# The sums of a block move into the weights' narrowing tile, the block tiles are loaded two blocks ahead, and the last weight pair is prepared in a fixed hand-out over four units

## The chip, the cores and the metric

The kernel runs on one core of one Trainium2 chip. The metric is the device time of one execution in microseconds. The time of a kernel is the median of several runs; a profiled execution is a run of its own, with its own time.

## The reference

Three stages follow one another. The change touches only the end of the third.

```python
# 1. retention (linear attention with decay), B, H, S, D = 4, 8, 768, 64
for t in range(S):
    state = gamma * state + einsum('bhd,bhe->bhde', k[:, :, t], v[:, :, t])
    y[:, :, t] = scale * einsum('bhd,bhde->bhe', q[:, :, t], state)
x = y.transpose(0, 2, 1, 3).reshape(3072, 512)
# 2. soft mixture of experts: 8 experts of 4 slots, softmax over tokens in, over slots out
logits = x @ phi
x = softmax_rows(logits) @ experts(softmax_columns(logits).T @ x)
# 3. two-layer network, 3072 tokens, 512 -> 2048 -> 512
h = x @ w_in
out = (h * sigmoid(1.702 * h)) @ w_out
```

## The kernel before

The third stage works on six blocks b = 0 to 5 of 512 tokens and on sixteen column groups of the 2048 hidden columns. A float32 product is split into high and low parts of a shorter type, and three matmuls (high by high, high by low, low by high) make one product.

The first column groups of each block are multiplied in the plain way, in the "plain units". Their result, 512 x 512 per block, goes by ScalarE into the tile stage and by DMA into a DRAM buffer parts[b].

The remaining column groups are taken in pairs r, one pair per "s-unit", and each pair is multiplied by a scheme of seven products instead of eight (the functions around s_unit, product and quad). There are 31 s-units n = 0 to 30: six per block in blocks 0 to 2, five in blocks 3 and 4, three in block 5. One s-unit is 42 matmuls of 128 x 256 (line 712) and two matmuls into the PSUM bank hb (line 678), which make the hidden values of the units that come next. ScalarE turns hb into the tile forms (line 680), casts the high parts ha and hs (line 696) and VectorE makes sums of forms and the low parts la and ls (line 673, the helper vadd). These are always one unit ahead of TensorE. The seven products of a block gather in PSUM over its units. In the last unit of a block VectorE and ScalarE combine them into the tile pt[b], which was loaded from parts[b]; the combination needs four sums e of 128 x 512, which are kept in a tile of their own, ev[b]. The first of them, e[:, 0], is a copy by ScalarE (line 756) that stands in the middle of the last unit, ahead of the cast of hs and of the next activation. The last four additions of a block, pt[b] plus a sum, are deferred: finish_block puts them on a list, and each of the block's successors' units takes one of them (in block 5 two). After the second and the fourth, store sends half a block, 512 KB, to the output.

The pool wq has three buffers (NQ = 3). They hold raw weights until VectorE has narrowed them, and after that the tiles pt and ev in turn. A new tile may be written only when every use of the tile that had the buffer has ended, DMA transfers too. All transfers of this stage are issued on SyncE's queue in the order in which the program names them.

The weights of pair 7, the last one, are prepared during the first s-units. VectorE narrows them into the tile wf["a"] (six instructions of lines 165 to 169), makes three sums, ScalarE casts two high halves (line 608) and VectorE subtracts two low halves (out tile wo_hl). What is emitted after which unit is set by work(budget), which takes from a queue until the costs written beside the items use up the budget of 1.7 (BUDS); after the fourth unit it takes all that is left. The tile wf["a"] serves pairs 2, 4, 6 and 7 and has no use after pair 7. Items of the list raws load the next raw tile each time that one has been narrowed; the last three items are load_part(0), make_ev(0) and load_part(1).

The order of instructions on each engine is the order in which the program is written.

Of the kernel before, what the change touches and what calls it, by code (L numbers as in the profile page):

```python
# [7 lines left out]
F32 = mybir.dt.float32  # L8
# [14 lines left out]
P = 128  # L23
# [9 lines left out]
NB = NT // 512  # L33
# [6 lines left out]
Q = 256  # L40
# [3 lines left out]
KA = (1, 256, 1, 512)  # L44
KW = (2, 1, 2)
BUD = 2.3
BUDS = 1.7
C1, C2 = 0.34, 0.6
WL = (3, 2)

# [2 lines left out]
def retention_soft_moe_mlp(  # L53
# [17 lines left out]
    def pool(stack, name, bufs, **kw):  # L71
        e = ctx.enter_context(ExitStack())
        kw.setdefault("reuse_waits", "tile")
        if "space" not in kw:
            kw["side"] = "left" if stack is left else "right"
        t = e.enter_context(tc.tile_pool(name=name, bufs=bufs, **kw))
        return t, e
# [7 lines left out]
    wq, wq_e = pool(left, "wq", NQ)  # L85
# [76 lines left out]
    def narrow(dst, raw):  # L162
        low, high = raw[..., 0], raw[..., 1]
        return [
            lambda: nc.vector.tensor_scalar(out=dst, in0=high, scalar1=3, scalar2=0x3FFFFFF8,
                                            op0=ALU.logical_shift_left, op1=ALU.bitwise_and),
            lambda: nc.vector.scalar_tensor_tensor(out=dst, in0=high, scalar=0xC0000000, in1=dst,
                                                   op0=ALU.bitwise_and, op1=ALU.bitwise_or),
            lambda: nc.vector.scalar_tensor_tensor(out=dst, in0=low, scalar=29, in1=dst,
                                                   op0=ALU.logical_shift_right, op1=ALU.bitwise_or),  # L170
        ]
# [419 lines left out]
    def pair_narrow(r, a):  # L591
        raw = wo_t[r].bitcast(U32).rearrange("p a (d z) -> p a d z", z=2)[:, a]
        w = wf["ab"[r in (3, 5)]][:, 2 * a:2 * a + 2].rearrange("p s d -> p (s d)")
        return narrow(w.bitcast(U32), raw)

    def pair_sums(r):
        w = wf["ab"[r in (3, 5)]]
        vadd(w[:, 4:6], w[:, 1:2].to_broadcast([P, 2, Q]), w[:, 0:4:3], ALU.subtract)
        vadd(w[:, 6], w[:, 3], w[:, 4], ALU.subtract)
        vadd(w[:, 7], w[:, 6], w[:, 2], ALU.subtract)  # L600

    def parts_of(r):
        return (slice(0, 4), slice(4, 8)) if r in FULL else (slice(0, 4, 2), slice(3, 6), slice(6, 8))
# [61 lines left out]
    span_ = [(NPL[b] // 2, 8 - NEND // 2 * (b == NB - 1)) for b in range(NB)]  # L665
    pairs = [(b, r) for b in range(NB) for r in range(*span_[b])]
    NS_ = len(pairs)
    AH, AL, pt, ev, PB = {}, {}, {}, {}, {}
    FT, deferred = [], []
    FORM = {"a": (1, 5), "s": (5, 8)}  # L670

    def vadd(out_, a, b_, op=ALU.add):
        nc.vector.tensor_tensor(out=out_, in0=a, in1=b_, op=op)  # L673
# [44 lines left out]
    def load_part(b):  # L718
        pt[b] = wq.tile([P, 4, DM], F32, tag="w", name=f"pt{b}")
        nc.sync.dma_start(out=pt[b], in_=parts[b])  # L720

    def make_ev(b):
        ev[b] = wq.tile([P, 4, 2, Q], F32, tag="w", name=f"ev{b}")

    def store(b, i):
        r0 = 512 * b + 256 - 256 * i
        nc.sync.dma_start(out=out[r0:r0 + 256].rearrange("(t p) d -> p t d", p=P), in_=pt[b][:, 2 - 2 * i:4 - 2 * i])

    def finish_block(b):
        e = ev[b]  # L730
        deferred.append(lambda: vadd(quad(b, 0, 0), quad(b, 0, 0), e[:, 0]))
        deferred.append(lambda: (vadd(quad(b, 0, 1), quad(b, 0, 1), e[:, 3]), b == NB - 1 or store(b, 0)))
        deferred.append(lambda: vadd(quad(b, 1, 0), quad(b, 1, 0), e[:, 2]))
        deferred.append(lambda: (vadd(quad(b, 1, 1), quad(b, 1, 1), e[:, 2]), b == NB - 1 or store(b, 1)))

    def s_unit(n):
        b, r = pairs[n]
        nxt, ends = n + 1 < NS_, r == span_[b][1] - 1
        e = ev.get(b)
        product(n, 2)  # L740
        if ends:
            vadd(quad(b, 0, 0), PB[2], quad(b, 0, 0))
        if nxt:
            s_h(n + 1, 1)
            s_sum1()
        else:
            end_h(1)
        product(n, 4)
        if ends:
            vadd(quad(b, 1, 0), quad(b, 1, 0), PB[4], ALU.subtract)  # L750
        if nxt:
            s_sum2()
            s_hi(n + 1, "a")
        product(n, 1)
        if ends:
            nc.scalar.copy(out=e[:, 0], in_=PB[1])
        if nxt:
            s_lo(n + 1, "a")
            s_hi(n + 1, "s")
        else:  # L760
            end_lo(0)
            end_lo(1)
        product(n, 7)
        product(n, 5)
        if nxt:
            s_lo(n + 1, "s")
        product(n, 6)
        if ends:
            vadd(e[:, 1], PB[6], e[:, 0])
            vadd(e[:, 2], PB[7], e[:, 1])  # L770
            vadd(e[:, 3], PB[5], e[:, 1])
            vadd(quad(b, 1, 1), PB[5], quad(b, 1, 1))
        if n + 2 < NS_:
            s_h(n + 2, 0)
        elif nxt:
            end_h(0)
        product(n, 3)
        if ends:
            vadd(quad(b, 0, 1), PB[3], quad(b, 0, 1))
            finish_block(b)  # L780
        else:
            for fn in deferred[:1 + (b == NB - 1)]:
                fn()
            del deferred[:1 + (b == NB - 1)]
# [54 lines left out]
    with tc.manual_schedule():  # L839
# [20 lines left out]
        for i in range(NI + 2):  # L860
# [16 lines left out]
            if i >= 2:  # L877
                n = i - 1
# [79 lines left out]
        wf = {"b": wp.tile([P, 8, Q], F32, tag="w", name="wfb")}  # L958
# [48 lines left out]
        raws = []  # L1007
# [1 line left out]
            raws += [("in", j, 0), ("in", j, 1), ("out", j + 1, 0)]  # L1009
        raws += [("out", r, 0) for r in range(5, 8)]  # L1010
        raws = [lambda x=x: load_raw(x) for x in raws]
        raws += [lambda: load_part(0), lambda: make_ev(0), lambda: load_part(1)]

        def next_raw():
            raws.pop(0)()
# [1 line left out]
        todo = []  # L1017
# [12 lines left out]
        def add_pair(r):  # L1030
            def make():
                for x, y, c in zip(pair_narrow(r, 0), pair_narrow(r, 1), (C1, C2, C2)):
                    queue.append((c, x))
                    queue.append((c, y))
                queue.append((0, next_raw))
                queue.append((2 * C2, lambda: (pair_sums(r), after(r))))

            def after(r):
                for x, sl in enumerate(parts_of(r)):
                    c = 1.2 if r in FULL else (0.6, 0.87, 0.6)[x]  # L1040
                    pend.append([1.6 + 0.8 * x, (0, lambda sl=sl: pair_hi(r, sl))])
                    pend.append([3.2 + 0.8 * x, (c, lambda sl=sl: pair_lo(r, sl))])

            todo.append(make)
# [30 lines left out]
        queue, pend, ready = [], [], []  # L1075

        def work(budget):
            while budget > 0:
                if not queue and not ready:
                    if todo:  # L1080
                        todo.pop()()
                    elif pend:
                        ready.append(pend.pop(0)[1])
                    else:
                        return
                c, fn = (ready or queue).pop(0)
                fn()
                budget -= c
                for p in pend:
                    p[0] -= c  # L1090
                ready.extend(p[1] for p in pend if p[0] <= 0)
                pend[:] = [p for p in pend if p[0] > 0]
# [28 lines left out]
        for u in range(5, NU + 2):  # L1121
            if u < NU:
                h_unit(u)
                lo_unit(u - 1)
                work(BUD)
            elif u == NU:
                lo_unit(u - 1)
                work(1000)
                assert len(raws) == 1, raws
                PB["h"] = pf.tile([P, 512], F32, tag="h", name="hb", bufs=3)  # L1130
                s_h(0, 0)
            else:
                s_h(0, 1)
                s_sum1()
                s_hi(0, "a")
                s_sum2()
                s_lo(0, "a")
                s_hi(0, "s")
                s_lo(0, "s")
                s_h(1, 0)  # L1140
            if u in (7, 8, 9):
                cp = tr_cT(u - 4, pf.tile([P, 4, P], F32R, tag="h", name=f"cp{u - 4}", bufs=3))
                copy_cT(u - 4, cp)
            o_unit(u - 2)
        for p, tag in ((2, "acc"), (4, "h"), (1, "h"), (7, "acc"), (5, "acc"), (6, "acc"), (3, "acc")):
            PB[p] = pf.tile([P, 2, Q], F32, tag=tag, name=f"P{p}", bufs=3 if tag == "h" else 5)
        add_pair(7)
        bh[7], bl[7] = [w_t[x].rearrange("p a b d -> p (a b d)").rearrange("p (s d) -> p s d", s=8) for x in range(2)]
        for n in range(NS_):
            b, r = pairs[n]  # L1150
            s_unit(n)
            work(BUDS if n < 3 else 1000)
            assert n < 4 or not (queue or todo or raws or pend or ready)
            if b > 0 and r == span_[b][0] + 1:
                make_ev(b)
                if b < NB - 1:
                    load_part(b + 1)
        end_units()


# [70 lines left out]
```

## Time and profile before

| | us |
|---|---|
| median of 3 runs | 467.64 |
| lowest and highest of the 3 | 466.35 and 469.69 |
| the profiled execution's own time | 465.35 |
| its span, first to last instruction | 463.6 |
| TensorE busy in the span | 441.0 (95%) |
| VectorE busy | 333.6 (72%) |
| ScalarE busy | 205.3 (44%) |

The share of TensorE is that of its matmul instructions over the whole program; matmuls overlap their successors, so the steps between them tell more than the share. The s-units lie between about 264 and 448 us of the span.

### The profile page before, as it was taken

The numbers are of one execution on the slowest core, as the hardware profiler recorded it, in microseconds if no ns is written. First come the engines' busy times: TensorE is split into PE (matmuls) and PEld (weight loads), VectorE is DVE, ScalarE is ACT, GpSimd is POOL, SyncE is SP. The second block draws the span as 40 slices with busy tenths as digits, with TensorE's granted clock in tenths as the row PEclk, the third lists the DMA queues.
The fourth block names the chain that finished last, engine by engine and source line by source line (L and its number), as shares of the span: only waits on it lengthen the run. The fifth ranks groups of instructions, "written<-read, shape, count | busy, mean of one in ns | idle before, by whom it ended". The sixth has DMA issues, their size and how long they took to land.

```text
span 463.6 us, 9973 instructions
## 1 busy us (share of the span) xinstructions
PE 441.0 (95%) x4130; PEld 367.0 (79%) x4130; DVE 333.6 (72%) x592; ACT 205.3 (44%) x351; POOL 48.3 (10%) x53
## 2 busy tenths in 40 slices
PE   8989999999999899999999999999999998797896
PEld 5777787786333577888888799999999998797895
DVE  2445675764374588897979698887887976775985
ACT  2223333233011356656376657565555553553530
POOL 3434435433000000000000000000000000000000
PEclk9999999999999999999999999999999999899799
DMA  8999999999899585973941500011213114014012
GB/s 300 408 402 403 398 385 387 379 404 353 311 426 379 213 299 203 308 248 144 322 143 55 181 3 1 1 45 52 86 45 96 43 47 135 2 45 137 20 72 91
DMA packets 27693, 92.40 MB, mean 199 GB/s; under 512 B 2880, under 2 KB 4320, under 8 KB 23296
## 3 DMA queue, kind: packets, MB, share of 16 engines
q1 hardware_dynamic: 27248, 91.24, 53.7%
q8 instruction: 32, 0.52, 0.5%
q10 hardware_dynamic: 288, 0.36, 0.3%
q0 software_dynamic: 112, 0.16, 0.1%
q14 instruction: 13, 0.11, 0.1%
HBM read 79.17 MB, written 12.58 MB: 198 GB/s over the span
## 4 chain that ended last, share of the span: by engine, by line
PE 76%; DMA 14%; DVE 4%; ACT 3%; issue 2%; POOL 1%; SPq 1%; DVEq 0%; ACTq 0%; POOLq 0%
PE P L712 29%; PE acc L649 17%; DMA qt<-qt_dram 9%; PE sc L213 3%; PE hb L678 3%; PE eo L513 3%; PE hp L488 3%; DMA out_dram<-pt 3%; PE y L262 3%; PE y L258 2%; PE P L825 2%; PE xp L283 2%; PE h L626 1%; DMA ktv_first<-ktv_dram 1%; PE op L369 1%
## 5 line engine op out<-in xcount | busy, mean ns | idle before, releaser
L673 DVE TENSOR_TENSOR forms<-forms 128x256 f32<-128x256 f32 (+1 forms) x93 | 47.6, 512 | 23.5 <-ACT forms L680 22.2
L712 PE MATMUL P<-bh,la 128*128 128x256 f32 x208 | 60.6, 291 | 0.3 <-DVE la L673 0.3
L680 ACT ACTIVATE forms<-hb 128x512 f32<-128x512 f32 x62 | 37.1, 598 | 53.6 <-PE hb L678 33.0
L649 PE MATMUL acc<-wo_hl,gh 128*128 128x512 f32 x192 | 59.9, 395 | 0.7 <-ACT gh L628 0.7
L712 PE MATMUL P<-bl,ha 128*128 128x256 f32 x208 | 60.2, 290 | 0.0
L712 PE MATMUL P<-bh,ha 128*128 128x256 f32 x208 | 60.1, 289 | 0.0
L712 PE MATMUL P<-bh,hs 128*128 128x256 f32 x156 | 44.4, 284 | 0.0
L712 PE MATMUL P<-bl,hs 128*128 128x256 f32 x156 | 44.2, 283 | 0.0
L712 PE MATMUL P<-bh,ls 128*128 128x256 f32 x156 | 44.2, 283 | 0.0
L217 DVE TENSOR_TENSOR pt<-sc,ca_t 128x512 f32<-128x512 f32 x44 | 28.3, 685 | 20.9 <-PE sc L213 20.9
L649 PEld LDWEIGHTS acc<-wo_hl,gh 128*128 128x128 f32 x192 | 35.3, 188 | 8.3 <-ACT gh L628 1.0
L712 PEld LDWEIGHTS P<-bl,ha 128*128 128x128 f32 x208 | 40.7, 196 | 1.2
L712 PEld LDWEIGHTS P<-bh,la 128*128 128x128 f32 x208 | 40.8, 196 | 0.5 <-DVE la L673 0.5
L712 PEld LDWEIGHTS P<-bh,ha 128*128 128x128 f32 x208 | 40.8, 196 | 0.0
L673 DVE TENSOR_TENSOR la<-forms,ha 128x1024 fp32r<-128x1024 f32 x31 | 37.9, 1222 | 0.0
L649 PE MATMUL acc<-wo_hl,gl 128*128 128x512 f32 x96 | 37.2, 392 | 0.5 <-DVE gl L636 0.5
L673 DVE TENSOR_TENSOR ls<-forms,hs 128x768 fp32r<-128x768 f32 x31 | 29.5, 952 | 10.9 <-ACT hs L696 10.9
L696 ACT CAST ha<-forms 128x1024 fp32r<-128x1024 f32 x31 | 32.6, 1052 | 8.6 <-DVE forms L673 7.7
L678 PE MATMUL hb<-cT,gst 128*128 128x512 f32 x62 | 25.7, 415 | 9.0 <-ACT forms L680 9.0
L628 ACT ACTIVATE gh<-h 128x512 fp32r<-128x512 f32 x30 | 18.0, 600 | 32.3 <-PE h L626 21.0
L712 PEld LDWEIGHTS P<-bl,hs 128*128 128x128 f32 x156 | 29.7, 191 | 1.2
L696 ACT CAST hs<-forms 128x768 fp32r<-128x768 f32 x31 | 25.9, 837 | 9.8 <-DVE forms L673 7.4
(224 smaller groups left out, 921.3 us busy)
## 6 DMA issues: line engine op xcount, KB each, us to landing
w<-w_dram SPq DMA_DIRECT2D x36, 512.0 KB, 7.5
w<-w_dram SPq DMA_DIRECT2D x14, 1024.0 KB, 8.5
ktv<-ktv_dram SPq DMA_DIRECT2D x20, 512.0 KB, 8.4
wi<-w_in_dram SPq DMA_DIRECT2D x7, 1024.0 KB, 5.3
wo<-w_out_dram SPq DMA_DIRECT2D x7, 1024.0 KB, 4.8
parts<-stage SPq DMA_DIRECT2D x24, 256.0 KB, 3.4
pt<-parts SPq DMA_DIRECT2D x6, 1024.0 KB, 6.0
qt<-qt_dram SPq DMA_DIRECT2D x21, 256.0 KB, 6.5
```

Source lines behind the costliest of these rows:

```text
L213: mm(sc[hh][:, a, :], lhsT=kT[hh * D:(hh + 1) * D, a, :], rhs=q_[hh * D:(hh + 1) * D, a, :], start=True, stop=True)
L217: nc.vector.tensor_tensor(out=pt[hh], in0=sc[hh], in1=mask[:, None, :].to_broadcast([P, NP, P]), op=ALU.mult)
L262: mm(out_(a, hh ^ (a & 1)), lhsT=vt[:, 2 * a + (hh ^ (a & 1)), :], rhs=pt[hh ^ (a & 1)][:, a, :], start=(c == 0 and a < 2), stop=True, ski ...
L488: mm(hp[32 * j:32 * j + 32, :], lhsT=slotT[:, k, :], rhs=w[:, j, :], start=(k == 0), stop=(k == KDM - 1))
L513: mm(op[32 * j:32 * j + 32, :], lhsT=hT[:, kk, 32 * j:32 * j + 32], rhs=w[:, j, :], start=(kk == 0), stop=(kk == 3))
L628: nc.scalar.activation(out=gh, in_=hp, func=AF.Gelu_apprx_sigmoid)
L649: mm(acc[t], lhsT=g[:, t * P:(t + 1) * P], rhs=w, start=f == f0 and n == 0, stop=f == f1 and n == 2)
L673: nc.vector.tensor_tensor(out=out_, in0=a, in1=b_, op=op)
L678: mm(PB["h"], lhsT=gst[:, f * P:(f + 1) * P], rhs=cT[:, 512 * b:512 * b + 512], start=True, stop=True)
L680: nc.scalar.activation(out=t[:, 3 * a:3 * a + 2].rearrange("p s d -> p (s d)"), in_=PB["h"], func=AF.Gelu_apprx_sigmoid)
L696: nc.scalar.copy(out=AH[n, k], in_=FT[0][:, c0:c1])
L712: mm(PB[p][:, t], lhsT=g[:, c], rhs=w, start=r == span_[b][0] and t == 0 and i == 0, stop=r == span_[b][1] - 1 and i == 2, skip_group_chec ...
```

## The change

Four things are changed. The sums e are kept in wf["a"] for every block, so that the tiles ev are gone. The pool wq thereby holds block tiles alone: pt[0], pt[1] and pt[2] are the last three items of raws, and pt[b + 2] is loaded in block b (b = 1 to 3) after its fourth unit, behind both stores of the block before, instead of pt[b + 1] after its second unit. The work on pair 7 is written out as four lists, one after each of the units 0 to 3. An assertion moves.

```diff
-    def make_ev(b):
-        ev[b] = wq.tile([P, 4, 2, Q], F32, tag="w", name=f"ev{b}")
...
     def finish_block(b):
-        e = ev[b]
+        e = wf["a"].rearrange("p (k t) d -> p k t d", t=2)
...
     def s_unit(n):
-        e = ev.get(b)
+        e = wf["a"].rearrange("p (k t) d -> p k t d", t=2)
...
-        raws += [lambda: load_part(0), lambda: make_ev(0), lambda: load_part(1)]
+        raws += [lambda: load_part(0), lambda: load_part(1), lambda: load_part(2)]
...
-        add_pair(7)
+        n7 = [x for p_ in zip(pair_narrow(7, 0), pair_narrow(7, 1)) for x in p_]
+        h7, l7 = [[lambda fn=fn, sl=sl: fn(7, sl) for sl in parts_of(7)] for fn in (pair_hi, pair_lo)]
+        tasks = [n7[0:4], n7[4:6] + [next_raw, lambda: pair_sums(7)], h7 + l7[0:1], l7[1:2]]
...
         for n in range(NS_):
             b, r = pairs[n]
             s_unit(n)
-            work(BUDS if n < 3 else 1000)
-            if b > 0 and r == span_[b][0] + 1:
-                make_ev(b)
-                if b < NB - 1:
-                    load_part(b + 1)
+            for fn in tasks.pop(0) if tasks else ():
+                fn()
+            if 0 < b < NB - 2 and r == span_[b][0] + 3:
+                load_part(b + 2)
```

On SyncE's queue, from the load of the first block tile to the second store of block 3, this stood before (parts is the DRAM buffer, pt the block tile, stage the tile of the plain results; the digit behind a name is the block, and the number after it that of the tile).

```order
L720 DMA pt0_3046<-parts0_60 128x2048
L661 DMA parts5_65<-stage_2136 128x512 x4
L720 DMA pt1_3371<-parts1_61 128x2048
L727 DMA out_dram<-pt0_3046 128x2x512
L720 DMA pt2_3734<-parts2_62 128x2048
L727 DMA out_dram<-pt0_3046 128x2x512
L727 DMA out_dram<-pt1_3371 128x2x512
L720 DMA pt3_4093<-parts3_63 128x2048
L727 DMA out_dram<-pt1_3371 128x2x512
L727 DMA out_dram<-pt2_3734 128x2x512
L720 DMA pt4_4452<-parts4_64 128x2048
L727 DMA out_dram<-pt2_3734 128x2x512
```

And this stands there now.

```order
L719 DMA pt0_3046<-parts0_60 128x2048
L719 DMA pt1_3105<-parts1_61 128x2048
L660 DMA parts5_65<-stage_2136 128x512 x4
L719 DMA pt2_3372<-parts2_62 128x2048
L723 DMA out_dram<-pt0_3046 128x2x512 x2
L719 DMA pt3_3851<-parts3_63 128x2048
L723 DMA out_dram<-pt1_3105 128x2x512 x2
L719 DMA pt4_4209<-parts4_64 128x2048
L723 DMA out_dram<-pt2_3372 128x2x512 x2
L719 DMA pt5_4567<-parts5_65 128x2048
L723 DMA out_dram<-pt3_3851 128x2x512 x2
```

A load of 1 MB no longer stands between the two stores of a block; the loads stand behind both, and that of pt1 has moved ahead of the last store into parts.

On VectorE, at the end of unit 2 and in unit 3, this stood before (wo_hl with wfa as an input is the low half of pair 7's weights; la and ls are the low parts of the next unit).

```order
L673 TENSOR_TENSOR forms_2264<-forms_2264 128x256
L673 TENSOR_TENSOR wo_hl1_2134<-wfa_2135,wo_hl0_2133 128x1024 x2
L673 TENSOR_TENSOR forms_2264<-forms_2264 128x512
L673 TENSOR_TENSOR forms_2264<-forms_2264 128x256
L673 TENSOR_TENSOR la_4_3461<-forms_2264,ha_4_3453 128x1024
L673 TENSOR_TENSOR ls_4_3477<-forms_2264,hs_4_3463 128x768
```

And this stands there now.

```order
L672 TENSOR_TENSOR wo_hl1_2134<-wfa_2135,wo_hl0_2133 128x1024
L672 TENSOR_TENSOR forms_2264<-forms_2264 128x512
L672 TENSOR_TENSOR forms_2264<-forms_2264 128x256
L672 TENSOR_TENSOR la_4_3461<-forms_2264,ha_4_3453 128x1024
L672 TENSOR_TENSOR ls_4_3477<-forms_2264,hs_4_3463 128x768
L672 TENSOR_TENSOR forms_2264<-forms_2264 128x256
L672 TENSOR_TENSOR wo_hl1_2134<-wfa_2135,wo_hl0_2133 128x1024
```

One of the two subtractions has moved behind the instructions of unit 3. Apart from it and the names of the tiles, the instructions of TensorE, VectorE, ScalarE and GpSimd stand in the order in which they stood.

## Rows read from the trace of the kernel before

**Rows 1.** The page, busy time of each engine.
```profile
PE 441.0 (95%) x4130; PEld 367.0 (79%) x4130; DVE 333.6 (72%) x592; ACT 205.3 (44%) x351; POOL 48.3 (10%) x53
```

**Rows 2.** Waits, 262 to 464 us: total us, times, longest us.
```profile
ACT ev L756 <- DMA out_dram<-pt: 12.2, 4, 5.8
...
PE hb L678 <- ACT forms L680: 8.3, 2, 4.2
```

**Rows 3.** Chain of waits, 375 to 464 us: start, us, what.
```profile
376.29 3.60 PE P L712 x30
...
386.63 0.70 DVE pt L673
...
387.39 0.34 SPq L720
...
387.77 6.87 DMA out_dram<-pt
...
397.18 5.09 PE P L712 x30
...
404.18 3.60 PE P L712 x30
...
409.68 3.60 PE P L712 x30
...
430.82 5.53 PE P L712 x30
...
438.26 3.60 PE P L712 x30
```

**Rows 4.** The page, DMA issues: KB each, median us from issue to landing.
```profile
pt<-parts SPq DMA_DIRECT2D x6, 1024.0 KB, 6.0
...
out_dram<-pt SPq DMA_DIRECT2D x10, 512.0 KB, 2.8
```

**Rows 5.** Timeline of ScalarE around the end of block 3: start, us, instruction [idle].
```profile
387.94 1.05 ACT L696 CAST ha<-forms 128x1024 fp32r<-128x1024 f32 x1
394.81 0.58 ACT L756 COPY ev<-P 128x512 f32<-128x512 f32 x1 [5.83 <-DMA out_dram<-pt]
```

**Rows 6.** Stretches: us, busy time of engines, granted clock, DMA share, GB/s.
```profile
292.00:386.00 94.00, 94.00 (x749) 91.93 (x748) 79.29 (x117) 53.74 (x72) 0.00 (x0) 1.00 0.15 51
391.65:403.06 11.41, 7.25 (x47) 6.96 (x45) 6.83 (x11) 4.49 (x7) 0.00 (x0) 0.85 0.18 68
...
425.03:437.14 12.11, 7.99 (x47) 7.64 (x45) 7.41 (x11) 4.81 (x7) 0.00 (x0) 0.72 0.16 60
```

**Rows 7.** Chain of waits, 262 to 345 us, units 2 to 7.
```profile
275.69 3.60 PE P L712 x30
...
282.98 1.22 DVE wo_hl L673
...
285.18 1.23 DVE la L673
...
287.65 3.60 PE P L712 x30
...
293.15 3.60 PE P L712 x30
...
298.65 3.60 PE P L712 x30
...
304.34 3.60 PE P L712 x30
```

**Rows 8.** Groups of VectorE by form, 292 to 386 us: count, busy us, mean ns, idle before.
```profile
L673 DVE TENSOR_TENSOR la<-forms,ha 128x1024 fp32r<-128x1024 f32 x17 | 20.8, 1223 | 0.0
L673 DVE TENSOR_TENSOR ls<-forms,hs 128x768 fp32r<-128x768 f32 x17 | 16.2, 952 | 0.0
L673 DVE TENSOR_TENSOR forms<-forms 128x256 f32<-128x256 f32 x34 | 14.4, 423 | 7.7 <-ACT forms L680 7.2
L673 DVE TENSOR_TENSOR forms<-forms 128x512 f32<-128x512 f32 x17 | 11.7, 691 | 5.9 <-ACT forms L680 5.6
```

More of the change, by code (lines that the diff above doesn't have):

```diff
@@ L46 @@
 BUD = 2.3
-BUDS = 1.7
 C1, C2 = 0.34, 0.6
@@ L667, in retention_soft_moe_mlp @@
     NS_ = len(pairs)
-    AH, AL, pt, ev, PB = {}, {}, {}, {}, {}
+    AH, AL, pt, PB = {}, {}, {}, {}
     FT, deferred = [], []
@@ L1128, in retention_soft_moe_mlp @@
                 work(1000)
-                assert len(raws) == 1, raws
+                assert len(raws) == 1 and not (queue or todo or pend or ready), raws
                 PB["h"] = pf.tile([P, 512], F32, tag="h", name="hb", bufs=3)
@@ L1151, in retention_soft_moe_mlp @@
             s_unit(n)
-            work(BUDS if n < 3 else 1000)
-            assert n < 4 or not (queue or todo or raws or pend or ready)
-            if b > 0 and r == span_[b][0] + 1:
-                make_ev(b)
-                if b < NB - 1:
-                    load_part(b + 1)
+            for fn in tasks.pop(0) if tasks else ():
+                fn()
+            if 0 < b < NB - 2 and r == span_[b][0] + 3:
+                load_part(b + 2)
         end_units()
```

## The prediction

> **What bounds the kernel now.** TensorE's matmuls cover 441.0 of 463.6 us [rows 1], so I looked for the stretches in which TensorE stops. The list of waits over the s-units shows two lines that belong together: ScalarE's copy into ev waited 12.2 us in four times for stores to land, the longest 5.8, and TensorE waited 8.3 us in two times for the activation that frees hb, 4.2 at most [rows 2]. The chain of waits, which I read next, links them. Its row of 30 matmuls starts once per unit, always at the same place of the unit, so the distance between two such rows is the time of a unit. Undisturbed it is 298.65 - 293.15 = 5.50 us [rows 7], and 409.68 - 404.18 = 5.50 far later [rows 3]. From 376.29 to 404.18 lie four units (20 to 23) and 27.89 us, 5.89 more than 4 x 5.50; from 409.68 to 438.26 lie four units (25 to 28) and 28.58 us, 6.58 more [rows 3]. These are the ends of blocks 3 and 4, the blocks of five units.
>
> The chain tells why. The fourth deferred addition of block 2 ends at 387.33 (386.63 + 0.70). It frees ev[2], whose buffer the load of pt[4] is waiting for, at the head of SyncE's queue; that load is issued at 387.39, and behind it the store of the second half of pt[2] at 387.77, which needs 6.87 us to land [rows 3] where the median store needs 2.8 and a block tile's load 6.0 [rows 4]. The sums of block 3 are to go into the buffer of pt[2]. So ScalarE's copy, for which it was free at 388.99 (387.94 + 1.05), starts at 394.81 [rows 5], and behind it on ScalarE stand the cast of hs, which VectorE needs for ls, and the activation that empties hb. TensorE runs on with what had been prepared and then stands still. Blocks 1 and 2 have one unit more between that store and the copy; their two waits are the rest of the 12.2 us, 0.6 together, and I count them as nothing.
>
> After both stops the matmuls are slow: 30 of them take 5.09 and 5.53 us instead of 3.60 [rows 3], 1.49 and 1.93 us more. The stretches that hold the stops show a granted clock of 0.85 and 0.72, the 94 us ahead of them 1.00 [rows 6]: part of the time went at 1.2 GHz instead of 2.4. The bill of both stops by its parts is 8.3 of standing and 3.42 of clock, 11.7 of the 12.47 us (5.89 + 6.58); the rest are hb matmuls at the lower clock.
>
> **The sums in wf["a"].** No instruction is added or removed by it. The copy now waits for the last use of wf["a"], which is VectorE's reading of the previous block's sums (the fourth deferred addition) and, for block 0, the last subtraction of pair 7 two units earlier. At the end of block 3 that addition was over at 387.33 and the copy could start at 388.99 [rows 3, 5]: 1.66 us of room. No transfer is left on which it depends. What is late next at a block's end is VectorE, which has seven more additions in the last unit. The three block ends without a long wait show what this costs: the unit from 298.65 to 304.34 took 5.69, 0.19 more than normal [rows 7]. I leave 0.19 at each of the two ends: 12.47 - 0.38 = 12.09 us gained. Bounds: 12.47 if nothing is left, and 6.5 if VectorE's whole lateness shows (first rival).
>
> Whether the 3.42 us of clock come back is part of that sum. I take them all, because in 94 us without a stop the clock stayed at 1.00 [rows 6]; without them the gain would be 9.4 us in all (third rival). The Trainium skill (TensorE: Matmul & The Clock Gate, section Why this matters for your kernels) states that an idle gap between bursts of matmuls sends TensorE back to half its rate. By that rule the whole of the clock part goes with the stops; the trace agrees, both stretches below 1.00 follow a stop.
>
> **The loads two blocks ahead.** Six loads as before. pt[b + 2] waits on SyncE's queue for both stores of pt[b - 1] to land, 2.8 us after the second one's issue at the median [rows 4]; behind it stand only the stores of the next units, the first of which is due three units (16 us) later or more. It is needed at the end of block b + 2, nine units or 49 us after its issue at the least, against 6.0 us of transfer. The load of pt[1] now goes ahead of the four stores of parts[5], waits only for pair 6's raw weights to be narrowed, and is needed 11 units into the stage; what it delays is a store into a buffer that is read some 100 us later. Cost of both: nothing; if a load did come late, VectorE's first addition of a block would wait for it, and 6.87 is the longest transfer in the rows [rows 3].
>
> **The work on pair 7.** The first three units keep what they had, except that one subtraction of 1.22 us leaves unit 2 for the end of unit 3. Before, units 2 and 3 together took 287.65 - 275.69 = 11.96 us, 0.96 over 2 x 5.50, and the unit after it was normal (293.15 - 287.65 = 5.50) [rows 7]. The chain runs there through the second subtraction (282.98, 1.22 us) and la (285.18, 1.23 us), for which TensorE waited until 286.4. Without it la ends about 1.2 us earlier, near 285.2; TensorE undelayed would ask for it just before 286 (its row of 30 would start at 275.69 + 11.00 = 286.69, and the first product of six matmuls and one of hb lie ahead of that). So the later part of the 0.96 goes; the earlier part, which lies ahead of the two subtractions and comes from the narrowing in units 0 and 1, stays. In unit 3 VectorE now has its normal 63.1 us / 17 = 3.71 (four groups [rows 8]) and 1.22, 4.93 of 5.50: it fits. I take 0.7; bounds 0 and 0.96.
>
> **Sum.** 12.09 + 0.7 = 12.8 us. The profiled execution took 465.35, so it would take 452.6. It was 2.3 below the median of the runs and 1.0 below the lowest; against the median the forecast is 467.64 - 12.8 = 454.8 us, 2.7% faster.
>
> **Rivals.** First, VectorE's lateness shows at the block ends once ScalarE's stop no longer hides it. A last unit holds 3.71 + 7 x 0.69 = 8.5 us of VectorE work in 5.50, 3.0 us too much. Elsewhere the next units win back 1.1 each (5.50 - 3.71 - 0.69); block 5 has two deferred additions per unit and wins back 0.4. If TensorE waited out all of it at both ends, 6.0 instead of 0.38, the gain is 7.2 and the time 460.4. Against it: the ends of blocks 0 to 2 have the same additions and cost about 0.2. It decides from some 1 us of wait per end.
>
> Second, the shared buffer becomes the wait: the copy of e[:, 0] stands behind VectorE's fourth deferred addition. It has 1.66 us of room; a VectorE that is 3.0 us late would stop ScalarE for 1.3 at each of two ends: 2.7 us lost, 457.5. For it speaks that blocks 3 and 4 have just one unit between that addition and the copy; against it, that two units of 1.1 us and more of catching up lie before.
>
> Third, the clock's part stays although the stops go: gain 9.4, 458.2. Against it stands the clock of 1.00 in the 94 us [rows 6].
>
> Fourth, the change doesn't do what it says, and the copy or something beside it on ScalarE waits as long for another transfer: only the 0.7 of pair 7 is won, 466.9. The named releaser in both long waits is a store from pt [rows 2, 5], and no store or load is left that touches wf["a"], so little speaks for it.
>
> Fifth, slower: a TensorE that no longer pauses for 180 us is put back to 1.2 GHz in the midst of the s-units. At half speed a unit costs up to 5.50 us more, so 2.3 units at that level use up the 12.8 us, and above 3.2 units (17.5 us lost) the kernel is over 1% slower, 472.3 or more. Against it: 94 us of full use at 1.00, and the fall comes after standing still, not after work [rows 6]. The same page of the Trainium skill, section What's actually happening, speaks against it too: activity is what releases the throttle.
>
> **How the numbers follow.** One per cent, 4.7 us, is about what a measurement of this kernel can tell from no change; the three runs of before lie within 0.7%. Chances: forecast 0.82; VectorE's lateness 0.05, shared buffer 0.04, clock part 0.04, all three still faster by over 1%; no effect 0.02; slower clock 0.03. So faster 0.95, same 0.02, slower 0.03. The range: at best all of the 0.96, all of the 12.47 and the 0.6 of the short waits come back, 14.0 us, on a run 1 us under the median as the lowest of before: 452.5. Upward it takes in the second and the third rival, 458.2, and a little of the runs' spread: 458.5. The first rival and the last two lie outside.
>
> **What the changed profile would show.** ScalarE's copy (now into wfa) without a transfer as releaser; TensorE's wait on the activation of hb in the last blocks gone or below 1 us; units 23 and 28 of 5.5 to 5.8 us between their rows of 30; a granted clock of 1.00 from 264 us to the end of the s-units; stores of 2.8 us; units 2 and 3 together near 11.2. The prediction is wrong if a block's end still costs over 1 us, if the chain passes through wfa or through a load of pt, or if the clock falls without a stop.

## The result and the profile after

The median fell from 467.81 us (466.35 to 469.69, 4 runs) to 453.39 us (452.46 to 455.17, 4 runs): a ratio of 0.9694 with an interval of 0.9644 to 0.9744, which is 14.4 us, between 12.0 and 16.7. The forecast was 454.8, in a range of 452.5 to 458.5.

The page of the changed kernel, against [rows 1 and 4]: busy time of each engine, the granted clock in 40 slices, and the block tiles' loads.

```profile
PE 437.0 (96%) x4130; PEld 363.4 (80%) x4130; DVE 332.2 (73%) x592; ACT 205.5 (45%) x351; POOL 48.3 (11%) x53
...
PEclk9999999999999999999999999999999999999999
...
pt<-parts SPq DMA_DIRECT2D x6, 1024.0 KB, 4.8
```

The numbers of instructions are the same. TensorE lost 4.0 us of busy time, and no slice has a lower clock any more. A block tile's load lands in 4.8 us instead of 6.0. The stores of half a block, seen from 262 to 452 us, keep their median:

```profile
out_dram<-pt SPq DMA_DIRECT2D x10, 512.0 KB, 2.8
```

The list of waits in the same stretch, against [rows 2]: total us, times, longest us.

```profile
ACT forms L679 <- PE hb L677: 34.9, 37, 2.1
...
PEld hb L677 <- ACT forms L679: 2.0, 7, 1.1
PE hb L677 <- ACT forms L679: 0.7, 1, 0.7
...
ACT wfa L752 <- PE P L711: 0.3, 1, 0.3
```

No line of this list names a transfer. ScalarE's copy, now into wfa, waited 0.3 us once, for a product, and TensorE's 8.3 us for the activation of hb have become 0.7, which lie ahead of the first s-unit (263 us).

The chain of waits around the ends of blocks 3 and 4, against [rows 3]: start, us, what.

```profile
378.33 3.60 PE P L711 x30
...
394.81 3.60 PE P L711 x30
...
400.06 0.45 PE hb L677
400.51 3.60 PE P L711 x30
...
406.00 3.60 PE P L711 x30
...
428.16 3.59 PE P L711 x30
```

A unit n is counted here from the start of its row of 30 matmuls to that of unit n + 1. Units 20 to 23 take 400.51 - 378.33 = 22.18 us where they took 27.89, and units 25 to 28 take 428.16 - 406.00 = 22.16 instead of 28.58: 5.71 and 6.42 back. All rows of 30 last 3.59 or 3.60. The same chain over units 2 and 3, against [rows 7]:

```profile
278.62 3.60 PE P L711 x30
...
284.35 3.59 PE P L711 x30
...
289.85 3.60 PE P L711 x30
```

289.85 - 278.62 = 11.23 us instead of 11.96: 0.73 back. From the first to the last matmul of the seven products the s-units took 184.48 us before (263.61 to 448.09) and take 171.44 now (266.54 to 437.97): 13.04 less, of which these three places are 12.86; another 0.14 is unit 18, 5.70 instead of 5.84 (the short wait at the end of block 2).

The spans of the two profiled executions differ by only 10.2 us (463.6 and 453.4), because the first s-unit begins 2.9 us later in the one shown of after. Over the eleven kernels of this text that start lies between 263.6 and 268.9 us, with the same work for the engines ahead of it. A span is therefore a poor measure of this change by itself; the length of the s-units is used below beside the times, and "lost" is always counted in it. The 14.4 of the medians is 1.4 over the 13.0, and the interval covers that.

The granted clock of the stretch from unit 5 to the end of the products, against [rows 6]:

```profile
293.70:437.90 144.20, 144.20 (x1150) 141.16 (x1150) 124.01 (x186) 82.29 (x110) 0.00 (x0) 1.00 0.16 59
```

### The profile page after: what moved, and what is told of

Same layout as the page of the kernel before. It is cut to its first block, busy times and chain, and to the rows that moved or that the text cites. A ratio compares the mean times of both kernels' runs of the same rounds, so it can differ in the third digit from the quotient of the medians.

```text
span 453.4 us, 9960 instructions
## 1 busy us (share of the span) xinstructions
PE 437.0 (96%) x4130; PEld 363.4 (80%) x4130; DVE 332.2 (73%) x592; ACT 205.5 (45%) x351; POOL 48.3 (11%) x53
## 4 chain that ended last, share of the span: by engine, by line
PE 85%; DMA 9%; DVE 3%; ACT 1%; issue 1%; SPq 0%; POOL 0%; DVEq 0%; ACTq 0%; POOLq 0%
PE P L711 34%; PE acc L648 17%; DMA qt<-qt_dram 8%; PE sc L212 4%; PE hb L677 4%; PE eo L512 3%; PE hp L487 3%; PE y L261 3%; PE y L257 2%; PE xp L282 2%; PE P L821 2%; PE op L368 1%; DMA ktv_first<-ktv_dram 1%; PE h L625 1%; PE st L269 1%; PE tq L523 1%
## 5 line engine op out<-in xcount | busy, mean ns | idle before, releaser
L711 PE MATMUL P<-bh,la 128*128 128x256 f32 x208 | 59.0, 283 | 0.0
L711 PE MATMUL P<-bl,ha 128*128 128x256 f32 x208 | 58.9, 283 | 0.0
L711 PE MATMUL P<-bh,ha 128*128 128x256 f32 x208 | 58.7, 282 | 0.0
L711 PEld LDWEIGHTS P<-bl,ha 128*128 128x128 f32 x208 | 39.4, 189 | 1.1
L711 PEld LDWEIGHTS P<-bh,ha 128*128 128x128 f32 x208 | 39.4, 190 | 0.0
L711 PEld LDWEIGHTS P<-bh,la 128*128 128x128 f32 x208 | 39.4, 189 | 0.0
L711 PEld LDWEIGHTS P<-bh,hs 128*128 128x128 f32 x156 | 29.5, 189 | 0.0
L711 PEld LDWEIGHTS P<-bh,ls 128*128 128x128 f32 x156 | 29.5, 189 | 0.0
```

What stands on the lines that cost most here:

```text
L711: mm(PB[p][:, t], lhsT=g[:, c], rhs=w, start=r == span_[b][0] and t == 0 and i == 0, stop=r == span_[b][1] - 1 and i == 2, skip_group_chec ...
```

## The experiments

The kernels e1 to e3 start from the kernel before and do one part of the change, or another in its place. The others start from the changed kernel and put a known stop back. Such a stop is a row of useless copies by ScalarE within the scratch tile stage; they are added work, and nothing is left out in any kernel. Each ratio is against the kernel before, timed in the same session.

**e1: the sums in wf["a"] alone.** The block tiles are loaded one block ahead, at the old place, and the work on pair 7 is dealt out by budget as before.

```diff
-        e = ev[b]
+        e = wf["a"].rearrange("p (k t) d -> p k t d", t=2)
...
-        raws += [lambda: load_part(0), lambda: make_ev(0), lambda: load_part(1)]
+        raws += [lambda: load_part(0), lambda: None, lambda: load_part(1)]
...
-                make_ev(b)
                 if b < NB - 1:
                     load_part(b + 1)
```

> The kernel before with one edit: the sums e are kept in wf["a"]; each block tile is still loaded one block ahead, between the two stores, and pair 7's work is dealt out as before. Theory (the copy's wait for a buffer of wq was the cost): both long stops go, units 20 to 23 and 25 to 28 take 22.2 us each instead of 27.9 and 28.6, units 2 and 3 together stay near 11.96, so 12.1 us less than before, about 455.7 against 467.8. Rival A (the loads two blocks ahead carry the gain): the stops stay, at or above 466. Rival B (a load between the stores costs something of its own): one or both of the ends keep 1 us or more, 457 or more.

Measured: 455.07 us (453.91 to 456.33) against 467.64, ratio 0.9714 (0.9653 to 0.9774). The s-units take 172.14 us, 12.34 less than before; no transfer stands among the waits, and units 2 and 3 keep their 11.95. Its chain at the two block ends:

```profile
382.54 3.60 PE P L712 x30
...
393.52 3.60 PE P L712 x30
...
399.21 3.59 PE P L712 x30
```

Both stops are gone by this part alone. The 0.70 us that separate it from the whole change in the s-units are those of units 2 and 3 (11.95 against 11.23), so nothing is left for the loads two blocks ahead.

**e2: the hand-out for pair 7 alone.**

```diff
-        add_pair(7)
+        n7 = [x for p_ in zip(pair_narrow(7, 0), pair_narrow(7, 1)) for x in p_]
+        h7, l7 = [[lambda fn=fn, sl=sl: fn(7, sl) for sl in parts_of(7)] for fn in (pair_hi, pair_lo)]
+        tasks = [n7[0:4], n7[4:6] + [next_raw, lambda: pair_sums(7)], h7 + l7[0:1], l7[1:2]]
...
-            work(BUDS if n < 3 else 1000)
+            for fn in tasks.pop(0) if tasks else ():
+                fn()
```

> The kernel before with one edit: pair 7's work in the fixed lists; sums and loads as before. Theory: units 2 and 3 together 11.2 us instead of 11.96, and both long stops stay (ScalarE's copy waits about 12 us in all for transfers, TensorE about 8 us for the activation of hb): 467.1 us by the sum, not to be told from 467.8 by one time. Rival (the hand-out shifts the phases of the later units): the two spans of four units differ from 27.9 and 28.6 by 1 us or more.

Measured, one run: 468.95 us, with a first s-unit at 268.9 us, the latest of all; its clock was at half speed twice ahead of this stage as well, for 3.4 us each, at 18.6 and 39.0 us. In the s-units, 182.78 us, the two stops stand as before; units 2 and 3 take 292.23 - 280.99 = 11.24, which is 0.72 less. The waits:

```profile
ACT ev L756 <- DMA out_dram<-pt: 11.8, 3, 5.8
...
PE hb L678 <- ACT forms L680: 9.0, 3, 4.2
```

The single time says nothing about 0.7 us; the chain does, and e1 against the changed kernel gives 0.72 from the other side.

**e3: the tiles ev stay in the shared buffers, but the load goes behind both stores.** This leaves the copy dependent on the store and takes away only what stands ahead of the store on SyncE's queue.

```diff
                 make_ev(b)
-                if b < NB - 1:
-                    load_part(b + 1)
+            if 0 < b < NB - 1 and r == span_[b][0] + 3:
+                load_part(b + 1)
```

> The kernel before with one edit: the load of the next block tile is emitted after a block's fourth unit, behind both stores, instead of after the second; the sums stay in ev, in a buffer of wq that the store must leave first. Theory (of the copy's 5.83 us of wait 4.07 came from the 1 MB load ahead of the store on SyncE's queue, 6.87 - 2.8): the store is issued near the fourth addition's end, lands 2.8 us later, and the copy waits about 1.3 us instead of 5.83. TensorE stood 4.2 us for a wait of 5.83, so it has 1.6 us in hand and does not stop: 12.1 us less than before, 455.7, with the buffer still shared. Rival A (any wait of the copy is paid): 1.3/5.83 of the stop stays, 12.1 - 2.7 = 9.4 less, 458.4. Rival B (the buffer, not the queue, is the cause, the store is slow in itself): about 467.

Measured: 457.14 us (456.09 to 457.86), ratio 0.9747 (0.9699 to 0.9795); s-units of 175.22 us, 9.26 less than before. ScalarE around the end of block 3, against [rows 5]:

```profile
388.55 1.06 ACT L696 CAST ha<-forms 128x1024 fp32r<-128x1024 f32 x1
391.43 0.59 ACT L756 COPY ev<-P 128x512 f32<-128x512 f32 x1 [1.82 <-DMA out_dram<-pt]
```

And SyncE's issues there (the store, then the load):

```profile
387.95 0.37 SPq L727 DMA_DIRECT2D out_dram<-pt  x1
388.43 0.41 SPq L720 DMA_DIRECT2D pt<-parts  x1
```

The store now goes out at once and lands in 3.37 us instead of 6.87 (387.95 to 391.32), and the copy waits 1.82 us instead of 5.83. At the end of block 4 it waits 1.73; there the list names VectorE's la, with which the copy shares no data and which ended in the same hundredth of a microsecond; the store had been issued 3.37 us before, so I take it to be the store again. The theory that such a wait is absorbed fell: TensorE lost 1.54 and 1.45 us at the two ends beyond the usual 0.2, and the gain of 9.26 is the one that the expectation gave for the other case. The clock stayed at 1.00 through all products. The chain shows where the loss came in:

```profile
393.65 0.70 DVE ev L673
394.35 0.02 issue
394.37 1.29 DVE ev L673 x2
...
398.25 1.15 DVE la L673
399.39 0.04 issue
399.44 0.74 PE P L712 x4
400.62 3.60 PE P L712 x30
```

TensorE waits for la of the next unit, behind VectorE's additions, which had been set back by the late copy and the late cast of hs. So what counts at a block's end is VectorE, and it has next to nothing in hand.

**e4 and e5: a stop of known length put back ahead of the copy, in blocks 3 and 4.**

```diff
+            if b in (3, 4):
+                for _ in range(12):        # e4; 6 in e5
+                    nc.scalar.copy(out=stage[:, 0], in_=stage[:, 1])
             nc.scalar.copy(out=e[:, 0], in_=PB[1])
```

> The changed kernel with 12 copies of 128x512 by ScalarE, of no use to the output, ahead of the copy of e[:, 0] at the ends of blocks 3 and 4, about 0.49 us each: ScalarE is held up 5.9 us at each, as the store held it up in the kernel before, with no transfer in it. Theory (a stop costs its standing time and then the lower clock): 6.3 us per end, 12.6 less or more by the phase of the clock, 453.4 + 12.6 = 466.0, with the granted clock below 1.00 after both stops and the rows of 30 matmuls at 5 us or more. Rival (standing alone is the cost, the clock fell for another reason): 453.4 + 2 x 4.2 = 461.8, clock at 1.00.

Measured: 469.97 us (468.52 to 471.81), ratio 1.0043 (1.0015 to 1.0072). The copies step by 0.65 us and not by the 0.49 I had reckoned with, so the cast of hs behind them started 7.5 us late and not the 5.9 of the expectation (7.6 in the later expectations, which also put six copies at 3.7 and three at 1.8; the trace has 3.6 and 1.6). This delay is called the hold. TensorE lost 7.62 and 8.58 us at the two ends, and the clock lay at 0.50 from 396.17 to 402.99:

```profile
396.17:402.99 6.82, 3.75 (x16) 3.66 (x17) 4.23 (x7) 3.92 (x8) 0.00 (x0) 0.50 0.00 0
```

A stop by ScalarE with no transfer in it thus brings back all of the time, and more because it is longer. The expected 466.0 was missed by 4.0 us, of which the two holds, mis-sized by some 1.6 each, account for 3.1.

> The changed kernel with 6 instead of 12 useless copies by ScalarE ahead of the copy of e[:, 0] at the ends of blocks 3 and 4; the twelve held ScalarE up for 7.6 us, so six hold it up for about 3.7. Theory A, that of the prediction (TensorE has 1.6 us in hand, and the rest of a stop's price is the clock): 3.7 - 1.6 = 2.1 us lost per end if the clock stays at 1.00, 453.4 + 4.2 = 457.6; one fall of the clock would add up to 1.7 each. Theory B, from the copy that waited 1.8 us and cost 1.5 at a clock of 1.00 (TensorE has 0.3 us in hand, because VectorE, with its seven additions, is late by as much as ScalarE was; the clock's part of a longer stop is mostly hidden behind that lateness): 3.4 us lost per end at any clock, 453.4 + 6.8 = 460.2.

Measured: 460.84 us (459.85 to 460.94), ratio 0.9832 (0.978 to 0.9885); s-units of 178.61 us, 7.17 more than the changed kernel's. The hold of 3.6 us cost 3.57 and 3.51 us. With 1.6 us in hand it would have cost 2.0 an end and whatever the clock adds. The clock fell here too, after waits of TensorE of 2.0 us at most:

```profile
387.00:395.00 8.00, 6.18 (x50) 5.88 (x49) 4.65 (x8) 6.84 (x11) 0.00 (x0) 1.00 0.55 196
395.00:398.00 3.00, 2.80 (x13) 2.75 (x14) 2.96 (x5) 0.75 (x2) 0.00 (x0) 0.60 0.01 3
```

So this kernel by itself doesn't tell a small stock of time from a clock that costs; e8 and e9 were made for that.

**e6: one of VectorE's seven additions put off into the next unit,** behind la, in the hope of the last 0.2 us at each block end.

```diff
-            vadd(quad(b, 0, 1), PB[3], quad(b, 0, 1))
+            late_add.append(lambda: vadd(quad(b, 0, 1), PB[3], quad(b, 0, 1)))
...
             s_lo(n + 1, "a")
+            while late_add:
+                late_add.pop()()
             s_hi(n + 1, "s")
```

> The changed kernel with the last of the seven additions of a block's end, pt plus PB[3], moved behind the subtraction that makes la in the next unit (for the last block it stays). Theory (the 0.2 us that each of five block ends still costs come from la of the following unit, late by VectorE's additions): units 7, 13, 19, 24 and 29 take 5.50 instead of 5.70, 1.0 us less in all, 452.4; no time can tell that for certain, the steps in the trace can. Rival (the additions are late whatever their order, and PB[3] now holds up the next product into it): the steps stay at 5.70 or grow, 453.4 to 454.4.

Measured: 459.31 us (457.63 to 462.35), ratio 0.9817 (0.9764 to 0.987), s-units 4.65 us longer than the changed kernel's. The units that were to take 5.50 (in the expectation 7, 13, 19, 24 and 29, counted by the row at which they end; 6, 12, 18, 23 and 28 as counted here) take 6.63 to 6.65 where the changed kernel has 5.70. The theory's step did not come, and the steps can't tell whether the 0.2 is gone beneath a larger wait. The waits, and the chain behind the end of block 0:

```profile
PEld P L711 <- DVE pt L672: 6.0, 5, 1.2
PE P L711 <- DVE pt L672: 4.4, 5, 0.9
```

```profile
302.46 1.14 DVE la L672
303.60 0.61 DVE pt L672
304.21 0.04 issue
304.25 1.69 PE P L711 x12
```

The put-off addition empties the PSUM bank PB[3], which the next unit's last product writes right behind its row of 30. That bank is the next wait, as the rival had it, but at 0.93 us net for each of five ends where the rival allowed 0.2.

**e7: the long stop in the middle of blocks 3 and 4,** in their third unit, behind the cast of ha, where no additions of a block's end follow.

```diff
             s_lo(n + 1, "a")
+            if b in (3, 4) and r == span_[b][0] + 2:
+                for _ in range(12):
+                    nc.scalar.copy(out=stage[:, 0], in_=stage[:, 1])
             s_hi(n + 1, "s")
```

> The changed kernel with 12 useless copies by ScalarE, 7.6 us, ahead of the cast of hs in the third unit of blocks 3 and 4, where VectorE has one deferred addition or none and is not late. At a block's end the same hold cost 7.6 and 8.6 us. Theory B (at a block's end the lower clock after the stop costs little, since VectorE's lateness would hold TensorE anyway): here TensorE stands for 7.6 less some 0.7 in hand, and then the slow matmuls come on top in full, 1.7 to 3 us, 8.6 to 9.9 lost per stop, 453.4 + 18.5 = 472 in one time. Rival (a stop costs its hold wherever it lies): 7 to 7.6 per stop, 468.

Measured, one run: 468.32 us, s-units of 187.32. The hold of 7.5 us cost 8.34 and 7.52, over units 20 and 21 and over 25 and 26, with TensorE standing up to 5.4 us at once and the clock at half speed after it, for 6.8 us each time. The figures lie between the two that were expected, and this kernel alone decides nothing.

**e8 and e9: short stops, in block 3 in mid-block, in block 4 at its end.** Three copies in e8, six in e9.

```diff
             s_lo(n + 1, "a")
+            if b == 3 and r == span_[b][0] + 2:
+                for _ in range(3):         # e8; 6 in e9
+                    nc.scalar.copy(out=stage[:, 0], in_=stage[:, 1])
             s_hi(n + 1, "s")
...
+            if b == 4:
+                for _ in range(3):         # e8; 6 in e9
+                    nc.scalar.copy(out=stage[:, 0], in_=stage[:, 1])
             nc.scalar.copy(out=e[:, 0], in_=PB[1])
```

> The changed kernel with 3 useless copies by ScalarE, about 1.8 us, at two places: ahead of the cast of hs in the third unit of block 3 (unit 20, VectorE not late) and ahead of the copy of e[:, 0] at the end of block 4 (unit 27). Theory B (at a block's end VectorE's additions leave TensorE 0.3 us in hand, in the middle of a block there are some 2 us, as 7.6 us of hold gave 5.5 of standing there): nothing lost after unit 20, and 1.5 us after unit 27, spread over units 28 and 29 beyond the 0.2 that they cost anyway, with the clock at 1.00 throughout. Theory A (TensorE has 1.6 us in hand at a block's end, as the standing of 4.2 us for a wait of 5.8 says): about 0.2 after unit 27 as well. If both places lose 1.5, the additions are not the reason.

> The same two places with 6 copies, about 3.7 us each. Theory B: after unit 27 3.5 us lost, as six copies cost at both block ends, and after unit 20 3.7 - 2.1 = 1.6 us if the clock stays at 1.00, or about 3 if it falls there. Theory A: 2.1 plus the clock's part at both places alike. The clock's own price shows in unit 20's place, where VectorE's lateness does not stand beside it: lost time minus 1.6.

Measured, one run each: 455.13 and 458.19 us; s-units of 172.92 and 176.59. In mid-block the hold of 1.6 us cost nothing and that of 3.5 cost 1.78; at the block's end they cost 1.45 and 3.42. From the chain of e9: the rows of units 19 and 21 to 23, and then those of units 25 and 29 around the end of block 4, with the wait for la ahead of the last.

```profile
370.64 3.60 PE P L711 x30
...
383.40 3.59 PE P L711 x30
388.90 3.60 PE P L711 x30
...
405.59 3.60 PE P L711 x30
...
428.79 1.15 DVE la L672
...
429.98 0.74 PE P L711 x4
...
431.16 3.59 PE P L711 x30
```

370.64 to 383.40 is two units and 1.8 us, and 405.59 to 431.16 is four units, the usual 0.2 and 3.4. All rows of 30 last 3.59 or 3.60, and the window of the s-units has the clock at full speed:

```profile
266.00:440.00 174.00, 170.00 (x1346) 165.50 (x1346) 148.03 (x222) 105.30 (x143) 0.00 (x0) 1.00 0.15 56
```

So a hold of 3.6 us at a block's end costs 3.42 without any loss of clock, and 3.57 and 3.51 with the clock at half speed for 3.4 us (e5). That separates the two terms.

The clock's stretches after the two stops of the kernel before, in the order of [rows 6], had unlike lengths:

```profile
397.55:400.96 3.41, 3.41 (x18) 3.41 (x18) 3.38 (x7) 1.17 (x2) 0.00 (x0) 0.50 0.00 0
428.27:435.10 6.83, 5.08 (x23) 4.98 (x24) 5.53 (x10) 3.43 (x6) 0.00 (x0) 0.50 0.00 1
```

All stops side by side. "Hold" is by how much later than in the changed kernel the cast of hs starts, counted from the unit's row of 30. "Lost" is TensorE's time beyond the 5.50 of a unit and the 0.2 of an undisturbed block end. "Slow work" is TensorE's busy time within the stretch at half clock; for the rest of the stretch it stood.

| kernel, place | hold, us | lost, us | clock after it | slow work, us |
|---|---|---|---|---|
| e3, ends of blocks 3 and 4 | 1.70, 1.60 | 1.54, 1.45 | full | none |
| e8, end of block 4 | 1.60 | 1.45 | full | none |
| e9, end of block 4 | 3.55 | 3.42 | full | none |
| e5, ends of blocks 3 and 4 | 3.56, 3.56 | 3.57, 3.51 | half for 3.4 us each | 3.41, 3.29 |
| before, ends of blocks 3 and 4 | 5.70, 5.66 | 5.71, 6.42 | half for 3.4 and 6.8 us | 3.41, 5.08 |
| e2, ends of blocks 3 and 4 | 5.67, 5.69 | 5.56, 5.70 | half for 3.4 us each | 3.13, 3.42 |
| e4, ends of blocks 3 and 4 | 7.46, 7.45 | 7.62, 8.58 | half for 6.8 us each | 3.75, 6.02 |
| e8, mid-block | 1.59 | 0 | full | none |
| e9, mid-block | 3.54 | 1.78 | full | none |
| e7, mid-block | 7.45, 7.45 | 8.34, 7.52 | half for 6.8 us each | 6.05, 4.19 |

At a block's end the loss at full clock is the hold less 0.15 (four stops, 0.13 to 0.16). In mid-block it is the hold less about 1.8 (one stop). At half clock the matmuls of the seven products start 0.21 us apart, here in the kernel before, where they start 0.12 apart at full clock (30 in 3.60):

```profile
398.52 0.41 PE L712 MATMUL P<-bh,ha 128*128 128x256 f32 x1
398.74 0.41 PE L712 MATMUL P<-bl,ha 128*128 128x256 f32 x1
```

Over all these stretches the mean is 0.213, so 0.44 of the slow work is time that the clock can add. With the two rules carried to the longer holds, which is an estimate, the other rows come out. In mid-block (e7) the loss beyond the hold less 1.8 is 2.7 and 1.8 us, and 0.44 of the slow work is 2.7 and 1.8 too: the clock is paid in full. At the eight block ends with slow work, 0.44 of it is 1.4 to 2.6 us, and the loss beyond the hold less 0.15 is smaller by 1.3 each time. That is the size of the second wait: after the stops at full clock, unit 23 or 28 takes 6.82 to 6.84 us, 1.3 more than 5.50 (e3, e8, e9). So the slow matmuls hide the second wait, and the clock costs only what goes beyond it. This also accounts for unlike losses after equal holds, 5.71 and 6.42 in the kernel before, and 7.62 and 8.58 in e4: the slow work differs.

## Why the prediction was right, and where its bill was not

**The sums in wf["a"].** Right in mechanism and size: 12.09 us were forecast, 5.71 + 6.42 = 12.13 came. That the copy's wait for a store in a shared buffer is the cause is shown from both sides: with the sums elsewhere and nothing else changed the stops go (e1), and a stop of ScalarE at that place that has nothing to do with DMA brings the time back (e4). The queue's order was most of the length of the wait, since a load put behind the store won 9.26 us (e3); the dependence itself is the other 3.

**The 0.19 left at each block end.** Right, 0.2 at all five ends. The trace of the changed kernel shows it, here behind the end of block 3:

```profile
398.05 1.22 DVE L672 TENSOR_TENSOR la<-forms,ha 128x1024 fp32r<-128x1024 f32 x1
399.36 0.60 ACT L679 ACTIVATE forms<-hb 128x512 f32<-128x512 f32 x1 [0.36 <-PE P L711]
400.01 0.19 PEld L677 LDWEIGHTS hb<-cT,gst 128*128 128x128 f32 x1 [0.16 <-ACT forms L679]
```

ScalarE's activation writes forms that VectorE's la still reads. It starts 0.09 us after la has ended (399.27), 4.72 us after the unit's row of 30, where one unit later it starts at 4.03; TensorE's next matmul into hb waits for it. The list names a product as releaser, with which the activation shares no data. All five ends show the same 4.62 for the end of la and 4.72 for the activation. In e6, with one addition less ahead of la, they are 4.22 and 4.32, and the activation is over at 4.91, ahead of the 5.25 at which an undisturbed unit starts that matmul. No run shows the unit at 5.50 by it, since e6 put another wait into the same unit. The first rival named a lateness that is real but costs 0.2 an end and not 3.0, as long as nothing else holds ScalarE up. The second rival's wait did not come: the copy into wfa waited for no deferred addition.

**The bill by parts failed in its split.** The prediction booked 8.3 us of standing and 3.42 of clock. The sum was right because it was read from the distance between rows of the chain, but the clock's 3.42, the excess of the two rows of 30, is not what the clock cost. By the table, the two holds at full clock would have cost 5.55 + 5.51 = 11.1 us of the 12.13 (an estimate from e3, e8 and e9); that leaves about 1.1 for the clock, and in e2 some 0.2. The reason, by the chains of e3, e5 and e9: a stop of ScalarE sets VectorE back too, and at a block's end VectorE has its seven additions still to do. At full clock TensorE first waits for the activation (2.0 us in e9) and then, one unit later, for VectorE, last for la; at half clock it works slowly through that second wait, and no wait for la stands in the chain of e5. The slow matmuls and the second wait lie on top of each other, so the bill counted as clock what would have been waiting. The table bears it out: at all eight block ends 1.3 us are hidden, the size of that wait, and in mid-block, where no additions follow, nothing is; e7 lost 8.34 and 7.52 where the hold less 1.8 is 5.7.

The Trainium skill (TensorE: Matmul & The Clock Gate, section Why this matters for your kernels) warns of throughput drops after idle gaps. That the clock falls after such gaps is what before, e2, e4, e5 and e7 show, where TensorE had waited 2.0 to 5.9 us; after the 2.0 us of e9 it did not fall. That a drop adds all of its slow work's extra time is not what e5 beside e9 shows.

For the same reason the third rival was no case of its own. Its gain of 9.4 us, everything but the clock, could not have come about: without the stops there is no low clock in the s-units (e1, and the changed kernel), and with them the clock is a small part. That e3's gain has the same size is chance; its loss is a wait at full clock.

**The loads two blocks ahead.** Nothing, as forecast (e1 against the changed kernel). The median load became 1.2 us shorter, off the path.

**Pair 7.** 0.7 forecast, 0.73 measured in the changed kernel and 0.72 in e2. The 0.23 us that remain in unit 2 (5.73) were not followed up.

**Against the medians.** 12.8 us were forecast and 13.0 came in the trace; the median moved by 14.4. The forecast was 1.4 us too high, which is within the interval and below the scatter of the first s-unit's start.

The signs named beforehand came as described: no transfer as releaser of the copy, TensorE's wait on hb below 1 us, units 23 and 28 of 5.71 and 5.70 us, a clock of 1.00, stores of 2.8 us, units 2 and 3 at 11.23.

## What to carry to other kernels

A tile that a compute engine writes should not take its buffer from a pool whose former tile still has to be stored: the engine then waits for a DMA, and everything that stands behind it on its queue waits too. If it must, put the store ahead of large loads on the same queue. And when a stop is to be priced, take the distance between repeated rows of the chain, not a sum of waits and slow matmuls: here a second engine's lateness lay under the slow matmuls, and the time in hand was 0.15 us at one place and 1.8 us a few units away.

## What was not expected of the hardware

- ScalarE's copies of 128 x 512 from SBUF to SBUF, one behind the other, step by 0.65 us (12 in 7.78), while the copy out of PSUM is followed by the next instruction after 0.49 (394.81 to 395.30 before). The source need not be the reason: the cast of hs, from SBUF to SBUF too, is followed after 0.73 with a duration of 0.83 (395.30 to 396.03), and the useless copies, unlike it, all write the same columns. No run varied that.
- A store of 512 KB with a load of 1 MB issued 0.48 us behind it on the same queue lands in 3.37 us, against 2.8 at the median and 6.87 with the load 0.38 us ahead of it.
- The clock fell after ScalarE's hold of 3.6 us at both block ends of e5 and not at that of e9, with the longest wait of TensorE 2.0 us in both. What tells the two apart stays open.
